# Batch 1's scores in float16 halves, batch 0's last 64 rows of two heads in one tile, and a new order

## The chip, the cores and the metric

The kernel runs on one core of one Trainium2 chip. The metric is device time in microseconds (us) of one execution. TensorE (PE) multiplies, VectorE (DVE), ScalarE (ACT) and GpSimd (POOL) work on tiles, and SyncE (SP) issues the transfers.

## The reference

```python
def _attn_ref(q, k, v):                       # each (4, 12, 448, 64) float32
    scores = 1.0 / np.sqrt(64) * np.matmul(q, k.transpose(0, 1, 3, 2))
    scores = np.where(np.triu(ones((448, 448)), k=1), -1e9, scores)
    scores = scores - np.max(scores, axis=-1, keepdims=True)
    attn = np.exp(scores)
    attn = attn / (np.sum(attn, axis=-1, keepdims=True) + 1e-09)
    return np.matmul(attn, v)

x = attn_out.transpose(0, 2, 1, 3).reshape(1792, 768)
r = np.maximum(x @ w_in, 0.0)                 # w_in (768, 2048)
out = (r * r) @ w_out                         # w_out (2048, 768)
```

Causal attention of 4 batches and 12 heads over 448 rows of 64 columns, then a feed-forward layer with a squared relu on all 1,792 rows.

## The kernel before

**Halves.** Most products run in float16 on values that are split in a high and a low half, three products for one (high by high, high by low, low by high). Scaling by powers of two from norms keeps the halves in range. `hi` (L478) writes a high half, as a rule on ACT (L485), `lo` (L491) the low half on DVE (L498). `pow2` (L508) makes a power of two and its inverse from a norm with four tiny DVE operations.

**Weights.** `load_wi` and `load_wo` (L999, L1006) bring w_in in 24 tiles and w_out in 16. `narrow` (L1011) repacks each on DVE in three operations (L1015, L1018, L1021). Gram matmuls of the packed tiles on PE (L1054, L1103; L1107 is the one of w_out) give the scale, `scale_out` (L1119) the scales of w_out, and then the halves are split (`split_pe` L1025, `split_w` L1038). The six tiles of one quarter of w_in's columns end in `widest` (L1066): a reduction (L1067) and a scaling of the identity (L1068) on DVE, then a matmul and a second reduction.

**Attention of batch 0** is `early` (L841), in float32: part 0 has the rows 0 to 255 in two chunks of 128, part 1 the rows 256 to 447 in two chunks of 96. For each of six pairs of heads q and k are transposed by PE (L877), scores (L898), the masked minimum with its accumulator on DVE (L906, a custom operation and the reading of its accumulator), exp on ACT (L910), normalisation, transposes (L938), weighted values (L954). Part 1 has 4 pieces for each pair, 352 or 448 columns wide.

**Attention of batches 1 to 3** is `pair` (L685), in four query chunks of 112 rows (`P`). Batches 2 and 3 split q and k in halves in the buffer `qs` and transpose them by transfers (L703) into `qk`; L770 are their scores, L753 their masked minima, L757 their exp. Batch 1 works in two parts of two chunks: `part_load` (L602) loads rows of q, k and v into `raw`; PE transposes q and k in float32 (L724, with `ident`), ACT copies them back over `raw` (L656); L784 are the float32 scores. In all batches but 0 the exponentials are split in halves in `psrc`, transposed by transfers (L678) into `pt`, and L816 are the weighted values with v's halves in `vp`, three products for two heads. L836 on POOL copies columns of the result `xt` for the next batch's blocks.

**Norms.** `vnorm` (L543) squares seven tiles `vn` of a batch's v on ACT (L552), with an accumulator. `pair_norm` does q and k of batches 2 and 3.

**Feed-forward.** `sub_block` (L1250) takes 256 or 128 rows: `prepare` (L1159) computes row norms (squares on ACT, L1168; the six pairs' squares added on DVE in three steps, L1171; the sum over columns on PE, L1174), the first layer is L1269, relu and square L1224 to L1233, the second layer L1287 in `second_layer` (L1278), with L1299 and L1310 scaling the results. Batch 0's two blocks are the phase "n", of 256 and 128 rows; the others are phase "m"; batch 3 goes through `products_block` (L1345).

**Order.** Nothing runs as it stands in the code. Each operation is added to a `Plan` (L94) with the tiles it reads and writes, one or more engines it can run on with a price, and a due time from the table PR (L23 to L77) by phase. `Plan.order` (L193) then schedules the list: whichever operation can start and is due first, on the engine that ends it first. `emit` (L290) writes the instructions in this order, so each engine's queue and SP's queue of transfers come from it. The code adds in this order: `early(0)`, `weights_in`, `early(1)`, `weights_out`, the blocks of batch 0, `attention(1)`, the blocks of batch 1, and so on (L1646 to L1671).

## Time and profile before

| | us |
|---|---|
| median of 3 runs (lowest, highest) | 618.01 (617.45, 620.81) |
| the profiled execution | 618.39 |
| its span | 616.7 |

| engine | busy us | share of the span |
|---|---|---|
| PE, matmuls | 597.9 | 97% |
| PE, weight loads | 442.2 | 72% |
| DVE | 497.4 | 81% |
| ACT | 428.6 | 69% |
| POOL | 9.7 | 2% |

The profile is one execution. Busy times are averages over stages that have different limits, so the windows of time further down are more telling. PE's matmuls are pipelined: the time of a group is best read from its start to the start of the next group. A weight load (PEld) overlaps matmuls. SP's rows show when transfers were issued, not how long they ran; the DMA share is the mean busy share of the core's 16 DMA engines.

### The profile page before, as it was taken

The page shows a single profiled execution, that of the slowest core. Times are in us where ns is not written, and L with a number is a line of the kernel's source. Part 1 is how long each engine was busy: PE and PEld are TensorE (multiplying, and loading weights), DVE is VectorE, ACT ScalarE, POOL GpSimd, SP SyncE. Part 2 cuts the span into 40 slices and gives each one's busy share as a digit, 9 for nine tenths or more (in the row PEclk, how much of TensorE's full clock was granted, in tenths as well). Part 3 has the DMA queues.
Part 4 walks back from the last instruction along what each step waited for, and adds up shares of the span by engine and source line. Part 5 has one row for each costly group of instructions (what it writes and reads, how often), then busy time and mean ns, then how long its engine had stood idle before and what let it go on. Part 6 is the DMA issues. An engine that isn't in the chain of part 4 may idle for free. (4 is left out here: it accounts for less than half of the span.)

```text
span 616.7 us, 13783 instructions
## 1 busy us (share of the span) xinstructions
PE 597.9 (97%) x5178; PEld 442.2 (72%) x5178; DVE 497.4 (81%) x1405; ACT 428.6 (69%) x1112; POOL 9.7 (2%) x21
## 2 busy tenths in 40 slices
PE   6888999999999999999999999999999999999997
PEld 4555778898566577868678668788966778886664
DVE  3799999999797798998889968889998999861000
ACT  4898999986798789577688869898934346451000
POOL 0000000001100000000000000000000000000000
PEclk9999999999999999999999999999999999999999
DMA  8965575765469788867789686775520000000000
GB/s 199 369 187 162 173 274 178 241 223 177 108 129 173 144 192 149 161 154 166 178 177 167 126 204 140 159 158 113 124 69 27 14 14 14 2 1 26 27 27 26
DMA packets 190914, 82.48 MB, mean 134 GB/s; under 512 B 177792, under 2 KB 185728, under 8 KB 190848
## 3 DMA queue, kind: packets, MB, share of 16 engines
q1 hardware_dynamic: 190704, 81.52, 53.7%
q8 instruction: 40, 0.66, 0.5%
q14 instruction: 26, 0.21, 0.1%
q10 hardware_dynamic: 144, 0.10, 0.0%
HBM read 47.19 MB, written 5.51 MB: 85 GB/s over the span
## 5 line engine op out<-in xcount | busy, mean ns | idle before, releaser
L1287 PE MATMUL bank<-wo,g 128*128 128x384 f16 x1056 | 182.2, 326 | 0.0
L1269 PE MATMUL bank<-xt,wi 128*128 128x256 f16 (+1 forms) x1728 | 169.1, 255 | 0.3 <-DVE xt L1191 0.3
L1269 PEld LDWEIGHTS <-wi 128*128 128x128 f16 x1728 | 144.6, 98 | 16.5 <-DVE psrc L498 0.7
L1287 PEld LDWEIGHTS <-g 128*128 128x128 f16 x1056 | 101.6, 98 | 63.0 <-issue 1.2
L757 ACT ACTIVATE pq<-bank,nm 112x336 f32<-112x336 f32 (+3 forms) x144 | 69.6, 492 | 14.6 <-DVE nm L753 14.0
L498 DVE SCALAR_TENSOR_TENSOR psrc<-pq,nm,psrc 112x112 f16<-112x112 f32 (+3 forms) x144 | 68.6, 506 | 8.4 <-ACT psrc L485 7.3
L485 ACT ACTIVATE psrc<-pq,nm 112x112 f16<-112x112 f32 (+3 forms) x144 | 67.0, 526 | 9.8 <-DMA pt<-psrc 6.9
L1310 DVE SCALAR_TENSOR_TENSOR ob<-bank,fac,ob 128x384 f32<-128x384 f32 (+1 forms) x27 | 16.1, 599 | 53.7 <-PE bank L1287 52.4
L1299 ACT ACTIVATE ob<-bank,fac 128x384 f32<-128x384 f32 x26 | 15.0, 576 | 59.3 <-PE bank L1287 59.1
L753 DVE CUSTOM_DVE_ANT_0 bank<-bank,mask,sc 112x112 f32<-112x112 f32 (+3 forms) x96 | 45.4, 512 | 7.0 <-PE bank L770 4.9
L816 PEld LDWEIGHTS <-vp 112*64 112x64 f16 x504 | 23.8, 109 | 12.4 <-issue 8.8
L770 PE MATMUL bank<-qk 128*112 128x112 f16 (+3 forms) x192 | 31.7, 285 | 0.7 <-ACT pq L757 0.6
L493 DVE TENSOR_TENSOR g<-r,g 128x512 f16<-128x512 f32 x44 | 30.1, 684 | 2.6 <-ACT g L485 2.4
L816 PE MATMUL bank<-pt,vp 112*64 112x224 f16 (+3 forms) x504 | 31.2, 268 | 0.6 <-DMA pt<-psrc 0.5
L1233 ACT ACTIVATE r<-r 128x512 f32<-128x512 f32 x40 | 24.9, 626 | 9.2 <-DVE r L1228 9.0
L1514 PEld LDWEIGHTS <-wi 128*128 128x128 f16 x288 | 28.1, 98 | 4.2 <-ACT g L1555 0.4
L757 ACT ACTIVATION_READ_ACCUMULATOR pq<-bank,nm 112x1 f32 x144 | 29.2, 203 | 0.0
L485 ACT ACTIVATE g<-r 128x512 f16<-128x512 f32 x44 | 27.0, 624 | 2.2 <-PE bank L1287 1.8
L906 DVE CUSTOM_DVE_ANT_0 bank<-bank,mask 128x128 f32<-128x128 f32 (+3 forms) x48 | 21.5, 487 | 4.3 <-PE bank L898 4.0
L898 PE MATMUL bank<-wo 64*96 64x256 f32 (+4 forms) x144 | 21.1, 389 | 2.8 <-ACT wo L656 2.0
L770 PEld LDWEIGHTS <-qk 128*112 128x112 f16 x192 | 19.8, 130 | 4.9 <-issue 1.1
L498 DVE SCALAR_TENSOR_TENSOR qs<-raw,sc,qs 112x512 f16<-112x512 f32 x24 | 17.3, 747 | 4.6 <-ACT qs L485 4.6
(189 smaller groups left out, 1023.2 us busy)
## 6 DMA issues: line engine op xcount, KB each, us to landing
raw<-in_moe_w_out_dram SPq DMA_DIRECT2D x8, 768.0 KB, 5.3
xt<-in_moe_w_out_dram SPq DMA_DIRECT2D x8, 768.0 KB, 4.6
xt<-in_moe_w_in_dram SPq DMA_DIRECT2D x11, 512.0 KB, 4.8
out_dram<-ob SPq DMA_DIRECT2D x25, 192.0 KB, 1.9
raw<-in_moe_w_in_dram SPq DMA_DIRECT2D x9, 512.0 KB, 5.4
vn<-in_v_dram SPq DMA_DIRECT2D x21, 192.0 KB, 3.8
raw<-in_v_dram SPq DMA_DIRECT2D x18, 224.0 KB, 3.2
raw<-in_q_dram SPq DMA_DIRECT2D x12, 224.0 KB, 3.4
```

The lines of the kernel that those rows point to most:

```text
L485: nc.scalar.activation(out=o, in_=i, func=ACTF.Copy, scale=s)
L493: return plan.add({"dve": dve_ns(n), "pool": pool2_ns(n)}, lambda e: engines[e].tensor_tensor(out=out(), in0=in_(), in1=top(), op=ALU.subt ...
L498: nc.vector.scalar_tensor_tensor(out=out(), in0=in_(), scalar=scale(), in1=top(), op0=ALU.mult, op1=ALU.subtract)
L753: one("dve", dve_ns(w, 1, 2 if F16S[b] else 1) - 10, lambda e: nc.vector.tensor_tensor_reduce(out=s.ap[0:P, 0:w], in0=s.ap[0:P, 0:w], in1= ...
L757: one("act", act_ns(w, True, 1, True), lambda e: nc.scalar.activation(out=p32[j].ap[0:P, b0 * P:b0 * P + w], in_=s.ap[0:P, 0:w], func=ACTF ...
L770: nc.tensor.matmul(out=s.ap[0:P, 0:(c + 1) * P], lhsT=qT.ap[:, j * NCH + c, :], rhs=kT.ap[:, a:a + c + 1, :].rearrange("p a t -> p (a t)") ...
L816: nc.tensor.matmul(out=pv.ap[j * D:(j + 1) * D, ca * P:t1], lhsT=vp.ap[:, hv, vb:vb + D], rhs=pT[j].ap[0:P, hp * ns + x:hp * ns + x + w, : ...
L906: one("dve", dve_ns(w, 1, 1) - 10, lambda e, c=c, j=j, w=w, ss=ss, nm=nm: nc.vector.tensor_tensor_reduce(out=ss[j].ap[0:M, 0:w], in0=ss[j] ...
L1233: nc.scalar.activation(out=r.ap[:, 0:n], in_=r.ap[:, 0:n], func=ACTF.Square)
L1269: nc.tensor.matmul(out=h.ap[:, y * n:(y + 1) * n], lhsT=wi_hl(ci, hw)[:, mc], rhs=x[:, kd, hx, off:off + n], start=(kd == 0 and hw == 0 an ...
L1287: nc.tensor.matmul(out=o.ap[:, 0:HALF], lhsT=gsl(kf, hg, tt * 128, (tt + 1) * 128), rhs=wo_hl(kf, hw)[:, hh * HALF:(hh + 1) * HALF], start ...
L1514: nc.tensor.matmul(out=ps.ap[:, y * n:(y + 1) * n], lhsT=A[0](f, kd, hw)[:, mc], rhs=B[0](kd, hx), start=(first and y == 0 and kd == 0 and ...
```

## The change

- **Batch 1's scores.** q and k of a pair are scaled by one power of two for all of q and one for all of k (`QK_UP`) and split in halves into `qs`; one transposing transfer for a pair and part brings both back into `raw`, 1,024 columns wide for the first part and 1,536 for the second, 12 in all. The scores are three float16 products. The PE transposes, ACT's copies and the float32 scores of batch 1 go. The loads of q and k are cut in smaller pieces.
- **Norms of batch 1.** `gram_norms(1)` loads q, k and v of batch 1 once more in 21 tiles and multiplies 63 blocks of 128 by 128 on PE; `vnorm(1)` goes.
- **Batch 0's last 192 rows.** A chunk of 128 rows for each head, 384 columns wide, and the last 64 rows of both heads stacked in one tile of 128 rows, 448 wide, with a mask of its own: 18 pieces for 24.
- **Small steps.** The low halves of batch 1's v are made on POOL, two operations each. In `widest` one multiplication replaces a reduction and a scaling. Scales of w_out that DVE made go to ACT. The squares of batch 0's blocks are summed by six matmuls instead of additions on DVE. Some results are staged in `xt` rather than in `qs`.
- **Order.** All of PR is new, and with it the order of the whole program. FIRST goes from 0 to 4: the first four loads of w_in have a due time of their own.

The core of the diff (PR, the cutting of the loads and the buffers left out):

```diff
-    FIRST = 0
+    FIRST = 4
-    KEYS = [(0, 128), (128, 128), (256, 96), (352, 96)]
+    KEYS = [(0, 128), (128, 128), (256, 128), (384, 64)]
...
+    def gram_norms(b):
...
+        for n, a in enumerate((q, k, v)):
...
+                    for z in range(w // 128):
+                        nc.tensor.matmul(
+                            out=ps.ap[:, n * 128:(n + 1) * 128], lhsT=top[:, z * 128:(z + 1) * 128], rhs=top[:, z * 128:(z + 1) * 128],
+                            start=(pr == 0 and z == 0), stop=(pr == NV - 1 and z == w // 128 - 1))
...
-                def turn(e, n=n, t=t, nch=nch):
-                    for c in range(nch):
-                        nc.tensor.transpose(t.ap[:, c * P:(c + 1) * P], (full(n) if nch == 4 else wide(n))[0:P, c], ident[0:P, 0:P])
...
-                one("pe", nch * 97, turn, raws[n][1] + ["ident"], [t], due)
-                copy(nch * P, lambda n=n: turned(n), lambda t=t, nch=nch: t.ap[:, 0:nch * P].rearrange("p (c t) -> p c t", t=P),
-                     [t], raws[n][1], due)
...
+                hi(nch * 128, lambda half=half: half(0), src, up, keys + [("vup", 1)], [(s_, n, 0)], due)
+                lo(nch * 128, lambda half=half: half(1), src, up, lambda half=half: half(0), keys + [("vup", 1), (s_, n, 0)], [(s_, n, 1)], due, keys)
+            o = at_[0][0] * 512 + at_[0][1] * 256
+            one("sp", {1024: 1540.0, 1536: 2200.0}[a], lambda e, a=a, o=o: nc.sync.dma_start_transpose(
+                out=raw[:, o:o + a // 2].bitcast(F16).rearrange("p (b t) -> p b t", t=128)[:, :, 0:P], in_=s_.ap[0:P]),
...
-                    for j in range(2):
-                        r = slice(j * D, (j + 1) * D)
-                        nc.tensor.matmul(
-                            out=ss[j].ap[0:P, 0:(c + 1) * P], lhsT=turned(0)[r, c - c0], rhs=turned(1)[r, 0:c + 1], start=True, stop=True)
+                    for z, (hq, hk) in enumerate(((0, 0), (0, 1), (1, 0))):
+                        for j in range(2):
+                            r = slice(j * D, (j + 1) * D)
+                            nc.tensor.matmul(
+                                out=ss[j].ap[0:P, 0:(c + 1) * P], lhsT=turned(0)[r, c - c0, hq], rhs=turned(1)[r, 0:c + 1, hk],
+                                start=(z == 0), stop=(z == 2))
...
-        T0, M, N = (0, 128, 256) if part == 0 else (256, 96, 192)
+        T0, MS, N = (0, (128, 128), 256) if part == 0 else (256, (128, 64), 192)
...
-            [], keys, ("wi", i - 60 * (i < FIRST), "wl"), 400.0, extra=1700.0)
+            [], keys, ("wi", i, "wl" if i >= FIRST else "wf"), 400.0, extra=1700.0)
...
+        for pr in range(0, NPAIR, 2):
+            one("act", act_ns(2 * n), lambda e, pr=pr: nc.scalar.activation(
...
+        for a, w, z in ((0, 3, 3), (0, 1, 1), (0, 1, 2)) if phase == "m" else ():
...
+        sums = 1 if phase == "m" else NPAIR
```

Three places of the new order. **At the start**, SP's queue of transfers (`wo` holds batch 0's q, k and v at this time, `g`, `xt` and `raw` are staging for w_in), before:

```order
L848 DMA wo<-in_k_dram 128x4x64 x2
L848 DMA wo<-in_q_dram 128x8x64 x2
L848 DMA wo<-in_k_dram 128x8x64 x2
L848 DMA wo<-in_v_dram 96x4x64 x2
L848 DMA wo<-in_v_dram 96x8x64 x2
L1002 DMA g<-in_moe_w_in_dram 128x1024 x4
L1002 DMA xt_140<-in_moe_w_in_dram 128x1024 x3
```

and after:

```order
L926 DMA wo<-in_k_dram 128x4x64 x2
L1118 DMA g<-in_moe_w_in_dram 128x1024 x3
L926 DMA wo<-in_q_dram 128x8x64 x2
L926 DMA wo<-in_k_dram 128x8x64 x2
L1118 DMA g<-in_moe_w_in_dram 128x1024
L1118 DMA xt_140<-in_moe_w_in_dram 128x1024 x3
L1118 DMA raw<-in_moe_w_in_dram 128x1024 x3
```

Three loads of w_in went ahead of q and k of the heads 4 to 11, and the rest of the first ones ahead of the later rows of v.

**Behind the last Gram matmul of w_out** (L1107 before, L1218 after), PE's queue, before:

```order
L1107 MATMUL bank_128<-wo 128x128
L1287 LDWEIGHTS g
L1287 MATMUL bank_120<-wo,g 128x384
L1287 LDWEIGHTS g
L1287 MATMUL bank_120<-wo,g 128x384
```

and after (L861 are batch 1's scores, L1385 the first layer):

```order
L1218 MATMUL bank_128<-wo 128x128
L861 LDWEIGHTS raw
L861 MATMUL bank_104<-raw 112x112
L861 LDWEIGHTS raw
L861 MATMUL bank_108<-raw 112x112
...
L1385 LDWEIGHTS wi
L1385 MATMUL bank_120<-xt_139,wi 128x128
```

Batch 1's first scores follow at once, and first-layer matmuls of batch 0's second block, which stood ahead of this place before, now follow it. Counted in the two programs: ahead of this place stood 288 first-layer matmuls of 256 columns, 288 of 128 and 54 second-layer ones; now 288, 90 and 24.

**POOL's queue**, where L836 alone worked in batch 1's attention before, has after:

```order
L526 TENSOR_SCALAR raw<-raw,vst 112x2x128
L528 TENSOR_TENSOR vp<-raw,vp 112x256
L914 TENSOR_SCALAR xt_140<-xt_139 128x2x64
...
L526 TENSOR_SCALAR raw<-raw,vst 112x512
L528 TENSOR_TENSOR vp<-raw,vp 112x512
```

L526 and L528 make a low half of v; there are twelve such couples, six of 256 columns and six of 512.

## Rows read from the trace of the kernel before

**Rows 1.** Windows: from:to, length, busy PE, PEld, DVE, ACT, POOL, PEclk, DMA share, GB/s
```profile
0.00:20.00 20.00, 13.77 (x64) 9.21 (x64) 5.92 (x33) 10.27 (x31) 1.38 (x9) 1.00 0.91 236
20.00:156.20 136.20, 130.08 (x1296) 101.23 (x1293) 134.33 (x358) 122.09 (x312) 4.77 (x6) 1.00 0.66 215
156.20:260.00 103.80, 101.61 (x881) 71.42 (x878) 88.83 (x281) 83.87 (x234) 0.37 (x1) 1.00 0.76 150
260.00:616.70 356.70, 352.40 (x2946) 260.34 (x2945) 268.36 (x737) 212.33 (x537) 3.23 (x6) 1.00 0.42 92
```

**Rows 2.** Timeline of PE at the last Gram matmuls: start, duration, line, out<-in
```profile
153.90 1.17 PE L1269 MATMUL bank<-xt,wi 128*128 128x128 f16 x18
154.90 1.14 PE L1287 MATMUL bank<-wo,g 128*128 128x384 f16 x6
155.88 0.51 PE L1107 MATMUL bank<-wo 128*128 128x128 bf16 x6
```

**Rows 3.** Timeline of PE in batch 1's scores, and weighted values of a later batch
```profile
167.71 0.83 PE L784 MATMUL bank<-raw 64*112 64x112 f32 x8
168.47 2.12 PE L1287 MATMUL bank<-wo,g 128*128 128x384 f16 x12
...
237.28 0.55 PE L724 MATMUL bank<-ident,raw 112*128 112x112 f32 x4
237.67 2.13 PE L1269 MATMUL bank<-xt,wi 128*128 128x256 f16 x18
239.73 1.57 PE L784 MATMUL bank<-raw 64*112 64x336 f32 x8
241.24 1.20 PE L816 MATMUL bank<-pt,vp 112*64 112x224 f16 x24
...
284.17 1.62 PE L816 MATMUL bank<-pt,vp 112*64 112x448 f16 x24
285.72 0.87 PE L770 MATMUL bank<-qk 128*112 128x336 f16 x4
```

**Rows 4.** Groups of DVE by shape: busy us, mean ns of one | idle before
```profile
L906 DVE CUSTOM_DVE_ANT_0 bank<-bank,mask 96x448 f32<-96x448 f32 x12 | 7.3, 640 | 0.0
L906 DVE CUSTOM_DVE_ANT_0 bank<-bank,mask 96x352 f32<-96x352 f32 x12 | 6.1, 542 | 0.0
...
L1171 DVE TENSOR_TENSOR sq<-sq 128x768 bf16<-128x768 bf16 x6 | 3.4, 568 | 0.0
...
L906 DVE DVE_READ_ACCUMULATOR2_ANT nm<- 96x1 f32 x24 | 3.3, 139 | 0.0
...
L1067 DVE TENSOR_REDUCE wst<-bank 128x1 f32<-128x128 f32 x4 | 1.1, 277 | 0.0
```

**Rows 5.** Timeline of DVE, the first narrowing, with its wait in brackets
```profile
18.01 0.43 DVE L1015 TENSOR_SCALAR wi<-g 128x512 int32<-128x512 int32 x1 [0.37 <-DMA g<-in_moe_w_in_dram]
```

**Rows 6.** Timeline of PE, two matmuls with 112-column weight loads and the next
```profile
288.39 0.26 PE L770 MATMUL bank<-qk 128*112 128x112 f16 x2
288.50 2.13 PE L1269 MATMUL bank<-xt,wi 128*128 128x256 f16 x18
```

**Rows 7.** Timeline of POOL beside DVE; POOL's L836 (min/median/max); a DVE group
```profile
287.38 0.74 DVE L498 SCALAR_TENSOR_TENSOR vp<-raw,vst,vp 112x512 f16<-112x512 f32 x1
287.62 0.66 POOL L836 TENSOR_SCALAR xt<-xt 128x128 f16<-128x128 f16 x1 [131.05 <-DVE xt L832]
...
L836 POOL TENSOR_SCALAR xt<-xt x12: 300/662/1080, 147.7 to 360.3; 128x128 f16<-128x128 f16 x12
...
L498 DVE SCALAR_TENSOR_TENSOR vp<-raw,vst,vp 112x256 f16<-112x256 f32 x6 | 2.8, 482 | 1.7 <-ACT vp L485 1.7
```

**Rows 8.** A window, SP's timeline in it, and landing times of L678's transfers
```profile
250.00:260.00 10.00, 10.00 (x106) 8.66 (x103) 9.26 (x22) 4.59 (x8) 0.00 (x0) 1.00 0.94 168
...
257.82 2.69 SPq L703 DMA_TRANSPOSE qk<-qs  x2
...
DMA to landing us min/median/max: 2.4/4.0/5.7
```

More of the change, by code (lines that the diff above doesn't have):

```diff
@@ L390, in attention_relu2_kernel, with n_ob @@
     b_ob = maker("ob", 2)
-    n_ob = lambda more, i: plan.spot([("qs", i - 2, 0), ("qs", i - 2, 1)], qs[:, i - 2, 0:2 * HALF].bitcast(F32)) if more and i > 1 else b_ob([128, HALF], F32)
+    def n_ob(more, i):
+        if more and i > 1:
+            prs = range(3 * i - 6, 3 * i - 3)
+            return xt[0][:, prs[0]:prs[-1] + 1, 0, 0:256].bitcast(F32), [("xt", 0, pr, 0) for pr in prs]
+        ob = b_ob([128, HALF], F32)
+        return ob, [ob]
     n_ss = maker("ss", 4)
@@ L712, in pair @@
             at_ = [place(pr, part, n) for n in range(3)]
-            raws = [(None, [("raw", z, h) for h in hs]) for z, _, hs in at_]
+            raws = [(None, [(k_, z, h) for h in hs for k_ in ("raw", "rawc")[:2 - (n > 0 and part)]]) for n, (z, _, hs) in enumerate(at_)]
+            nchs = [4 if part and n else 2 for n in range(3)]
             row = lambda n: raw[:, at_[n][0] * 512:(at_[n][0] + 1) * 512]
+            half_row = lambda n: row(n)[:, 0:512] if nchs[n] == 4 else row(n)[:, 256 * at_[n][1]:256 * (at_[n][1] + 1)]
@@ L730, in pair @@
+            raws[2] = (row(2)[0:P] if part else wide(2)[0:P], raws[2][1])
         z = None if whole or c0 else pr % 2
@@ new lines, in turned_qk @@
+            qkk = early_keys(0, part, pr) + early_keys(1, part, pr)
+            one("pe", 2 * 0.86 * sum(MS), turn, qkk + ["ident"], [t], due)
+            if part == 0:
+                copy(512, lambda: rows[:, :, part].rearrange("p n c t -> p c n t"),
+                     lambda t=t: t.ap.rearrange("p (c n t) -> p c n t", n=2, c=2), [t], qkk, due)
+                return rows, qkk
+            for c, M in enumerate(MS):
+                copy(2 * M, lambda c=c, M=M: rows[:, :, part, c, 0:M],
+                     lambda t=t, c=c, M=M: t.ap[:, 256 * c:256 * c + 2 * M].rearrange("p (n t) -> p n t", n=2),
+                     [t], early_keys(0, part, pr, (c,)) + early_keys(1, part, pr, (c,)), due)
@@ new lines, in scored @@
+        def scored(pr):
+            rows, qkk = turned_qk(pr)
+            nm, sm = n_nm([128, 8], I32), n_sm([128, 8], I32)
+            if part == 0:
+                p32, pT = [[mk(j) for j in range(2)] for mk in (lambda j: n_ep(0, j, pr % 3), lambda j: n_eT(j, pr % 3))]
+                pieces = [(p32[j], (p32[j], c), [0, 128][c], 128 * (c + 1), 2 * j + c) for c in range(2) for j in range(2)]
+            else:
+                p32, pT = [n_ep(1, None, pr % 3)], [n_eT(None, pr % 3)]
+                pieces = [(p32[0], (p32[0], j), 384 * j, 384, j) for j in range(2)] + [(p32[0], (p32[0], 2), 768, 448, 2)]
+            held[pr] = p32, nm, sm, pT, pieces
@@ L898, in scores @@
                             nc.tensor.matmul(
[L899 to L900 removed]
+                                out=ss[j].ap[o, a:a + n_], lhsT=rows[r, 0, part, c, 0:MS[c]],
+                                rhs=rhs, start=(z == 0), stop=(z == len(blocks) - 1))
                 one("pe", mm32_ns(w) + 95, scores, qkk + [k_ for z in range(part) for k_ in early_keys(1, z, pr)], ss,
@@ L1173, in prepare, with total @@
                 [(sqs, i) for i in range(z, z + w)] + [(sqs, i) for i in range(a, a + w)], [(sqs, i) for i in range(a, a + w)], due, port=True)
-        one("pe", mm_ns(n), lambda e: nc.tensor.matmul(
-            out=tot.ap[:, 0:n], lhsT=ones_b, rhs=sq[:, 0, 0:n], start=True, stop=True), [(sqs, 0)], [tot], due)
+        sums = 1 if phase == "m" else NPAIR
+        def total(e):
+            for i in range(sums):
+                nc.tensor.matmul(out=tot.ap[:, 0:n], lhsT=ones_b, rhs=sq[:, i, 0:n], start=(i == 0), stop=(i == sums - 1))
+        one("pe", sums * mm_ns(n), total, [(sqs, i) for i in range(sums)], [tot], due)
         u, sg = n_u([128, SUB], I32), n_sg([128, SUB], F16)
@@ L1613, in attention @@
             return
+        vnorm(b)
         for i in pairs:
@@ L1630, in consts @@
             fill=-float(2 ** 100), base=0, channel_multiplier=1)
+        nc.vector.memset(mask2.ap[:, 0:384], 0.0)
+        for j in range(2):
+            h = slice(j * 64, (j + 1) * 64)
+            nc.gpsimd.tensor_copy(out=mask2.ap[h, 384:448], in_=mask[h, MZ + j * 64:MZ + (j + 1) * 64])
         nc.gpsimd.memset(ident, 1.0)
```

385 lines of the change are left out of this document (225 added, 160 removed), and 50 rows, old and new, of the table PR.

## The prediction, made before the changed kernel was run

> **What bounds the kernel now.** I read the windows first [rows 1], because what limits the kernel differs by stage. The column to compare is each engine's busy time against the window's length, and after it DMA's share. In the first 20 us DMA is at 0.91 while DVE works 5.92 us: everything waits for data. From 20 to 156.2 us DVE is busy 134.33 of 136.2, which makes it the bound, with PE (130.08) and ACT (122.09) behind it. From 156.2 on PE is the bound: 101.61 of 103.8 us, then 352.40 of 356.7, at a granted clock of 1.00 (the level of 2.4 GHz) throughout. I therefore cut the program at 156.2 us. There the last Gram matmul of w_out ends [rows 2], the last thing that the weights' preparation on DVE releases on PE. Ahead of this marker the time is set by when DVE gets through the weights and batch 0's softmax; behind it by how much PE work is left: 616.7 - 156.2 = 460.5 us.
>
> After that I read PE's timeline where batch 1's scores are computed [rows 3], DVE's groups by shape [rows 4], and for what can go wrong the first narrowing [rows 5], a 112-column weight load [rows 6], POOL beside DVE [rows 7] and the DMA share with the transposing transfers [rows 8].
>
> **PE behind the marker, what goes.** Batch 1 has six head pairs. Each has ten fp32 transposes, and four of them delay the next matmul by 237.67 - 237.28 = 0.39 us, 97 ns each [rows 3]: 60 x 97 = 5.8 us. Its fp32 scores come in two visits: the narrow widths cost 168.47 - 167.71 = 0.76 us, the wide ones 241.24 - 239.73 = 1.51 us [rows 3], so 2.27 x 6 = 13.6 us. Together 19.4 us.
>
> **What comes.** Three float16 products for two heads and four query chunks, widths 112 to 448: 24 matmuls a pair. The trace has a twin with the same widths and count, the weighted values of a later batch: 24 matmuls from 284.17 to 285.72, 1.55 us [rows 3]. 1.55 x 6 = 9.3 us. The twin splits the array by output columns, the new scores by input rows; the old fp32 scores split it by rows too, so overlap of the two heads is likely. If they did not overlap, 18 matmuls of 256 columns in 239.73 - 237.67 = 2.06 us [rows 3] give 0.45 ns a column, and 6 x 1,120 columns x 6 pairs would be 18.0 us. So the saving lies between 1.4 and 10.1 us; I take 10.1, the nearer row.
>
> Here is where a weight load could decide. Two matmuls with their own 112-column loads start at 288.39, and the next matmul starts 0.11 us later [rows 6]; such loads are thus mostly hidden. The Trainium skill, page "TensorE: Matmul & The Clock Gate", section "LDWEIGHTS (loading the stationary operand)", gives a load as columns / 1.2 ns, 93 ns for 112. If every load stood in line, 144 of them would take 13.4 us instead of 9.3, and the sum below would end 4.1 us later; the 0.11 us for two speaks against it here.
>
> **What moves.** The program's order shows PE work that stood ahead of the marker and now stands behind it: 198 first-layer matmuls of 128 columns and 30 second-layer ones of 384. Eighteen of the first take 154.90 - 153.90 = 1.00 us, six of the second 155.88 - 154.90 = 0.98 [rows 2]. 198 x 55.6 ns + 30 x 163 ns = 11.0 + 4.9 = 15.9 us more behind the marker. So the stretch behind it becomes 460.5 + 15.9 - 10.1 = 466.3 us, **5.8 us longer**. The change can pay only if the marker comes more than 5.8 us earlier.
>
> **DVE ahead of the marker.** The 24 softmax reductions of batch 0's last 192 rows cost 12 x 640 + 12 x 542 + 24 x 139 ns = 17.5 us [rows 4]. The 18 new ones are six of 448 columns and twelve of 384; with 640 for the first and 575 between the two rows for the second, 6 x 640 + 12 x 575 + 18 x 139 = 13.2 us: -4.3. The six additions of squares for batch 0's blocks go to PE: 768 columns take 568 ns [rows 4], and they have 1,920 columns in all: -1.4. Four reductions of 277 ns go [rows 4]: -1.1. Twelve tiny operations on the scales go to ACT, at some 139 ns: -1.7. Four low halves of q and k come ahead of the marker, 4 x 0.48 [rows 7], and three of g leave it, a little wider: nil. That is 8.5 us by durations. Neighbouring records overlap by some hundredths, so I take 8. DVE is 98.6% busy here, so this should come through, unless ACT or PE is the next one late. ACT is handed work (the scales, the new high halves) but loses batch 1's squares of v, which the 63 Gram matmuls replace. These cost PE 63 x 55.6 ns = 3.5 us, which the 15.9 us that left this stretch cover.
>
> **The start.** The w_in loads stand behind q and k of batch 0's first 256 rows and all of its v on the queue. The first narrowing waits for its load until 18.01 us [rows 5], and DVE idles 14 of the first 20 us [rows 1]. Three loads now go ahead of q and k of heads 4 to 11 and of the later rows of v, together 1.64 MB (from the shapes), 6.9 us at the 236 GB/s of this window. DVE then has weights to narrow in its gaps from about 11 us on. The price: these q and k loads land later by 3 x 0.26 MB, 3.3 us, so pairs two to five of batch 0 start later. The gain can be at most the idle left between 11 and 20 us, about 6, and nothing if DVE waits for q and k instead. I take 4. If there is a loss I expect it under 1 us, because DVE's queue has narrowing to do meanwhile.
>
> **The sum.** The marker comes 8 + 4 = 12 us earlier, at 144; the stretch behind it is 466.3 us. Span 616.7 - 12 + 5.8 = 610.5; the profiled execution took 618.39, 1.7 more than its span, so 612.2. The median of the runs shown (618.01) lies 0.4 below the profiled one: **611.8 us**, 1.0% faster. About 0.5% (3.1 us) is what a measurement of this kernel can tell from no change: faster means under 614.9, slower over 621.1.
>
> **Rivals.**
> 1. *The transfers become the bound (slower).* Twelve transposing transfers, six of 1,024 and six of 1,536 columns, join the queue in the stretch of batch 1's attention, where DMA is at 0.76 of 103.8 us, 78.9 us [rows 1]. In 250 to 260 us six of the smaller kind are issued (two queue operations a row, three such rows) at a share of 0.94 [rows 8]: at most 9.4 / 6 = 1.6 us each. 6 x 1.6 + 6 x 2.4 = 24 gives 103 of 103.8 + 5.8 = 109.6 us: it fits, barely. If each held the engines for the 4.0 us from issue to landing [rows 8], 78.9 + 48 exceeds the stretch by 17.3 us: 629. It decides from (109.6 - 78.9) / 15 = 2.0 us a smaller one. PE behind it can take first-layer work of batch 1's neighbours meanwhile, so a part is hidden.
> 2. *The relief doesn't bring the marker forward.* ACT is busy 122.09 of 136.2 us and PE 130.08 [rows 1]; if one of them, or the w_out loads, sets the marker, each us missing from the 12 is lost. Without any of it 611.8 + 12 = 624; slower from a marker less than 2.7 us earlier, within 0.5% up to 8.9.
> 3. *Only the start fails.* The marker is 8 us earlier: 616, no difference.
> 4. *POOL holds DVE up.* POOL gets 24 operations, the low halves of batch 1's v. The one POOL row beside a DVE operation took 0.66 us and ended as DVE's did (287.62 + 0.66 against 287.38 + 0.74), where the shortest took 300 ns for 128 columns [rows 7]: one waits for the other. At 300 ns per 128 columns they hold 12 x 0.6 + 12 x 1.2 = 21.6 us. DVE idles 15 us in the stretch [rows 1] and gains as much from new low halves as the stretch grows by (24 come, 12 go: 12 x 0.48 = 5.8). If all of it blocked DVE, 6.6 us would be lost: 618, no difference. The Trainium skill, page "SBUF — State Buffer", section "Who interferes with whom", says that a DVE operation with two SBUF inputs and a GpSimd one that reads SBUF block each other fully; the two ends above agree with it.
> 5. *The heads don't overlap on PE*, or weight loads show: 8.7 us lost at most, 620; no difference for most of that range.
>
> **How the numbers follow.** Forecast with its own spread of some 4 us either way (607 to 615): 0.56. Both relief terms better than taken (marker 14 us earlier and fewer gaps on PE, under 607): 0.06. Rival 1: 0.09, most of it slower. Rival 2: 0.13, two thirds of it slower. Rival 3: 0.06; rival 4: 0.05; rival 5: 0.05. Faster 0.62, within 0.5% 0.21, slower 0.17. The range leaves out the best 0.05 or so and the tails of rivals 1 and 2: 605 to 622.
>
> **What would show it.** The last Gram matmul of w_out near 144 us (rival 2: after 150); the first narrowing near 11 us; DVE still near 98% busy up to the marker; groups of score matmuls adding up to 1.55 us a pair (rival 5: 3.0); DMA under 0.95 in the stretch of batch 1's attention and PE at 98% there (rival 1: PE gaps that end with a transposing transfer); DVE operations lengthened beside POOL's (rival 4). I am wrong if the marker stays where it is, or if PE gets gaps behind it that were not there.

## The result, and the profile after

The changed kernel takes **625.12 us** (median; 624.98 to 627.77) against 617.73 (617.35 to 620.81) of the kernel before on the same chip: a ratio of **1.0119**, 95% interval 1.0077 to 1.0161. It is 7.4 us slower, where 611.8 was forecast. The profiled execution of after took 627.77 us with a span of 626.1, 2.65 more than the median; its granted clock was 0.995, that of its other executions 0.997 to 1.00.

The windows of after, cut as in [rows 1] at the end of the last Gram matmul of w_out, its "marker" (from:to, length, busy PE, PEld, DVE, ACT, POOL, granted clock, DMA share, GB/s):

```profile
0.00:20.00 20.00, 13.46 (x60) 8.62 (x62) 9.55 (x39) 9.07 (x27) 1.90 (x11) 1.00 0.90 243
20.00:153.60 133.60, 126.50 (x1143) 95.31 (x1139) 123.97 (x316) 108.33 (x260) 3.75 (x4) 0.99 0.73 228
153.60:260.00 106.40, 100.72 (x993) 71.88 (x991) 87.10 (x261) 87.22 (x237) 7.15 (x15) 0.98 0.79 166
260.00:626.10 366.10, 361.78 (x3051) 269.25 (x3048) 276.19 (x769) 220.64 (x546) 14.17 (x18) 1.00 0.45 97
```

Its PE timeline at the marker, as in [rows 2], and its DVE timeline at the first narrowing, as in [rows 5] (start, duration; in brackets the wait and what ended it):

```profile
153.31 0.51 PE L1218 MATMUL bank<-wo 128*128 128x128 bf16 x6
```
```profile
11.16 0.43 DVE L1131 TENSOR_SCALAR wi<-g 128x512 int32<-128x512 int32 x1 [2.04 <-DMA g<-in_moe_w_in_dram]
```

The marker, at the cut of [rows 1], came 2.6 us earlier (156.2 to 153.6), not 12, and the stretch behind it grew by 12.0 us (616.7 - 156.2 = 460.5 to 626.1 - 153.6 = 472.5), not by 5.8. All of these are of the one profiled execution, so the 2.65 us that it lies above the median are in them. DVE's account up to the marker, from the first two windows and [rows 1]:

| us | before | after | forecast |
|---|---|---|---|
| DVE work up to the marker | 140.25 | 133.52 | -8; came -6.7 |
| of it done in the first 20 us | 5.92 | 9.55 | +4; came +3.6 |
| DVE idle from 20 us to the marker | 1.87 | 9.63 | no change; came +7.8 |

-6.7 - 3.6 + 7.8 is the 2.6. Both gains of DVE were there, nearly in full. What they freed turned into DVE standing idle. What DVE waited for most, from 20 us to the marker of after (total us, times, longest us), and the longest of these waits:

```profile
DVE bank L975 <- PE bank L1006: 4.5, 5, 2.3
```
```profile
21.54 0.30 DVE L975 CUSTOM_DVE_ANT_0 bank<-bank,mask 128x128 f32<-128x128 f32 x1 [2.29 <-PE bank L1006]
```

L1006 are batch 0's scores, L975 their masked minima: DVE waits for scores five times. Its longest single wait, 2.86 us for ACT, is shown below with the Gram matmuls. The experiments ask what stands behind these waits. Markers of experiments below are the end of the last row of that kind: 155.88 + 0.51 = 156.4 us before, 153.31 + 0.51 = 153.8 after.

Groups of PE by shape that waited for a transfer behind the marker (busy us, mean ns | idle us before, and what ended it), first of before, then of after:

```profile
L816 PE MATMUL bank<-pt,vp 112*64 112x224 f16 x216 | 15.2, 261 | 0.5 <-DMA pt<-psrc 0.5
```
```profile
L894 PE MATMUL bank<-pt,vp 112*64 112x224 f16 x216 | 15.2, 262 | 2.9 <-DMA pt<-psrc 2.9
...
L894 PE MATMUL bank<-pt,vp 112*64 112x448 f16 x72 | 9.6, 360 | 0.6 <-DMA pt<-psrc 0.6
...
L861 PE MATMUL bank<-raw 64*112 64x336 f16 x36 | 3.8, 317 | 0.8 <-DMA raw<-qs 0.8
```

L861 are the new scores, which wait for the new transposing transfer (`raw<-qs`), and L894 (L816 before) the weighted values, which wait for the old one of the softmax weights (`pt<-psrc`).

### The profile page after: what moved, and what is told of

It reads as the page before. It is cut to its first block, busy times and chain, and to the rows that moved or that the text cites. A ratio compares the mean times of both kernels' runs of the same rounds, so it can differ in the third digit from the quotient of the medians.

```text
span 626.1 us, 13955 instructions
## 1 busy us (share of the span) xinstructions
PE 602.5 (96%) x5239; PEld 445.1 (71%) x5239; DVE 496.8 (79%) x1383; ACT 425.3 (68%) x1068; POOL 27.0 (4%) x47
## 4 chain that ended last, share of the span: by engine, by line
PE 63%; DMA 3%; DVE 2%; ACT 2%; issue 1%; DVEq 0%; SPq 0%
PE bank L1403 29%; PE bank L1385 17%; PE bank L1633 9%; PE bank L894 4%; PE bank L846 4%; DMA pt<-psrc 1%; DMA out_dram<-ob 1%; PE bank L861 1%; ACT pq L833 1%; DMA raw<-qs 1%; DVE bank L829 0%; ACT psrc L510 0%; DVE psrc L523 0%; ACT junk L577 0%; DVE qs L523 0%
## 5 line engine op out<-in xcount | busy, mean ns | idle before, releaser
L1385 PE MATMUL bank<-xt,wi 128*128 128x256 f16 (+1 forms) x1728 | 167.7, 256 | 0.7 <-ACT r L1342 0.7
L1385 PEld LDWEIGHTS <-wi 128*128 128x128 f16 x1728 | 145.0, 98 | 17.4 <-issue 2.2
L833 ACT ACTIVATE pq<-bank,nm 112x112 f32<-112x112 f32 (+3 forms) x144 | 69.5, 489 | 14.5 <-DVE nm L829 12.1
L523 DVE SCALAR_TENSOR_TENSOR psrc<-pq,nm,psrc 112x112 f16<-112x112 f32 (+3 forms) x144 | 66.9, 504 | 5.3 <-ACT psrc L510 5.0
L510 ACT ACTIVATE psrc<-pq,nm 112x112 f16<-112x112 f32 (+3 forms) x144 | 64.6, 523 | 4.7 <-DMA pt<-psrc 2.0
L829 DVE CUSTOM_DVE_ANT_0 bank<-bank,mask,sc 112x336 f32<-112x336 f32 (+2 forms) x96 | 45.7, 511 | 7.9 <-PE bank L846 7.0
L894 PE MATMUL bank<-pt,vp 112*64 112x224 f16 (+3 forms) x504 | 31.1, 268 | 3.5 <-DMA pt<-psrc 3.5
L894 PEld LDWEIGHTS <-vp 112*64 112x64 f16 x504 | 23.8, 109 | 13.8 <-issue 6.9
L846 PE MATMUL bank<-qk 128*112 128x336 f16 (+3 forms) x192 | 31.7, 284 | 0.0
L526 POOL TENSOR_SCALAR raw<-raw,vst 112x256 f32<-112x256 f32 (+1 forms) x12 | 8.7, 724 | 410.8 <-ACT vp L510 381.5
L1006 PE MATMUL bank<-wo 64*128 64x128 f32 (+4 forms) x168 | 23.1, 359 | 2.6 <-ACT wo L726 2.0
L846 PEld LDWEIGHTS <-qk 128*112 128x112 f16 x192 | 21.2, 130 | 5.0 <-DMA qk<-qk 0.3
L829 DVE CUSTOM_DVE_ANT_0 bank<-bank,mask,vst 112x112 f32<-112x112 f32 (+3 forms) x48 | 22.2, 512 | 0.8 <-PE bank L861 0.8
```

The costliest lines, as they stand in the source:

```text
L510: nc.scalar.activation(out=o, in_=i, func=ACTF.Copy, scale=s)
L523: nc.vector.scalar_tensor_tensor(out=out(), in0=in_(), scalar=scale(), in1=top(), op0=ALU.mult, op1=ALU.subtract)
L829: one("dve", dve_ns(w, 1, 2) - 52, lambda e: nc.vector.tensor_tensor_reduce(out=s.ap[0:P, 0:w], in0=s.ap[0:P, 0:w], in1=mask[0:P, MZ + P - ...
L833: one("act", act_ns(w, True, 1, True), lambda e: nc.scalar.activation(out=p32[j].ap[0:P, b0 * P:b0 * P + w], in_=s.ap[0:P, 0:w], func=ACTF ...
L846: nc.tensor.matmul(out=s.ap[0:P, 0:(c + 1) * P], lhsT=qT.ap[:, j * NCH + c, :], rhs=kT.ap[:, a:a + c + 1, :].rearrange("p a t -> p (a t)") ...
L894: nc.tensor.matmul(out=pv.ap[j * D:(j + 1) * D, ca * P:t1], lhsT=vp.ap[:, hv, vb:vb + D], rhs=pT[j].ap[0:P, hp * ns + x:hp * ns + x + w, : ...
```

## The experiments

Five questions, each with a theory and its opposite: do the new Gram matmuls hold PE's queue, do the transposing transfers hold it, does relief of DVE bring the marker forward at all, is the earlier start worth its 4 us, and does POOL hold DVE. Each marker is read from one execution. Names with a_ are edits of the changed kernel, with b_ of the kernel before. Ratios are against the kernel before.

### The Gram matmuls' loads

a_gram_free: the Gram matmuls read a constant tile, so that they wait for no load. a_gram_noload leaves out their 21 loads too.

```diff
-  lhsT=top[:, z * 128:(z + 1) * 128], rhs=top[:, z * 128:(z + 1) * 128],
+  lhsT=ones_b, rhs=ones_b,
```
```diff
-  one("sp", dma_ns(128 * w * 4, w * 4), lambda e, ...: nc.sync.dma_start(out=t.ap, in_=...), ...
+  one("sp", dma_ns(128 * w * 4, w * 4), lambda e: None, ...
```

> The changed kernel in the same order, but the 63 Gram matmuls of batch 1's norms read a resident tile of ones, so they wait for no load (the norms are not the true ones); the loads still run. Theory 1 (a Gram matmul that waits in PE's queue for its load stops the first layer behind it, and the clock falls): the marker comes 3 to 5 us earlier than 153.6 and the time falls to 620 to 622. Theory 2 (ahead of the marker the relief of DVE ends in the chain of batch 0's last rows): 624 to 626, no difference.

> As the one before, and the 21 loads for these norms are left out. If the loads' time on the queue and on the DMA engines delays w_out's loads, this is 2 to 4 us faster than with the loads; if not, the same within 1 us.

Measured: 620.97 us, 1.0057 [1.0036, 1.0079], marker 149.4; and 621.54, 1.0063 [1.0041, 1.0085], marker 149.3. By medians the wait costs 4.1 us of the time, where the interval just overlaps that of after (1.0077 to 1.0161); the loads themselves cost nothing that shows. PE's timeline at the first of these matmuls (L596), of after and then of a_gram_free:

```profile
122.58 0.52 PE L1218 MATMUL bank<-wo 128*128 128x128 bf16 x6
124.74 0.35 PE L596 MATMUL bank<-vn 128*128 128x128 bf16 x3 [1.64 <-DMA vn<-in_k_dram]
...
126.11 5.42 PE L1385 MATMUL bank<-xt,wi 128*128 128x256 f16 x36
131.36 0.51 PE L596 MATMUL bank<-vn 128*128 128x128 bf16 x6
```
```profile
121.28 0.52 PE L1218 MATMUL bank<-wo 128*128 128x128 bf16 x6
121.64 0.33 PE L596 MATMUL bank<-ones_b 128*128 128x128 bf16 x3
```

At the marker the two executions are 4.4 us apart. Of this, 122.58 - 121.28 = 1.3 us were there ahead of the wait, and 1.3 are first-layer matmuls that ran slower behind it (5.42 us for 36, above, against 4.09). In a_plain_copy (next part), whose Gram matmuls wait too, they ran at full pace:

```profile
124.59 0.35 PE L596 MATMUL bank<-vn 128*128 128x128 bf16 x3 [1.05 <-DMA vn<-in_k_dram]
...
125.67 4.09 PE L1385 MATMUL bank<-xt,wi 128*128 128x256 f16 x36
```

The wait stands in PE's queue ahead of w_out's Gram matmuls and of the first layer, and the engines that wait for PE stood still with it. ACT's timeline of after a few us later, and DVE's next wait:

```profile
129.60 0.60 ACT L1342 ACTIVATE r<-bank 128x512 f32<-128x512 f32 x1 [4.06 <-PE bank L1385]
```
```profile
131.05 1.02 DVE L523 SCALAR_TENSOR_TENSOR wo<-wo,wst 128x768 f16<-128x768 f32 x1 [2.86 <-ACT wo L510]
```

### The transposing transfers

a_plain_copy moves batch 1's q and k with plain transfers of the same tiles in the same places, so that they arrive untransposed; the second head's score matmuls then read 48 rows for 64. a_both is a_plain_copy and a_gram_free together.

```diff
-  nc.sync.dma_start_transpose(out=raw[:, o:o + a // 2].bitcast(F16).rearrange(...)[:, :, 0:P], in_=s_.ap[0:P])
+  nc.sync.dma_start(out=raw[0:P, o:o + a // 2].bitcast(F16), in_=s_.ap[0:P])
```

> The changed kernel in the same order, but the 12 transposing transfers of batch 1's q and k are plain copies of the same bytes from the same tile to the same place (the scores are not the true ones, and the second head's matmuls read 48 rows for 64). Rival 1 (the transposing transfers fill the DMA engines and delay the exponentials' transfers, so that PE waits at 190 to 201 us): PE's gaps between the marker and 260 us fall by 4 us or more and the time to about 621. If not: 624 to 626.

> The changed kernel in the same order with both edits: Gram matmuls of batch 1's norms on a resident tile, and plain copies for the 12 transposing transfers. If the two waits are separate losses they add up: 625.1 - 4.1 - 3.2 = 617.8. If the second only shows because the first came ahead of it: about 620.5.

Measured: a_plain_copy 621.88 us, 1.0079 [1.0051, 1.0106]; a_both 619.30, 1.0018 [1.0001, 1.0035], marker 150.0, and behind it 617.1 - 150.0 = 467.1 us. By medians the transposing kind costs 3.2 us alone, inside the intervals' overlap, and 1.7 where the Gram matmuls don't wait (a_gram_free against a_both), where the intervals just part. Read the other way, the Gram matmuls' wait costs 621.88 - 619.30 = 2.6 us where the transfers are plain, with intervals well apart. So the two cost 5.8 us together (625.12 to 619.30), and how they share it depends on which goes first. PE at the longest gap of this stretch, of after and then of a_plain_copy:

```profile
190.51 3.10 PE L1403 MATMUL bank<-wo,g 128*128 128x384 f16 x18
195.80 0.62 PE L894 MATMUL bank<-pt,vp 112*64 112x224 f16 x12 [2.19 <-DMA pt<-psrc]
196.35 4.78 PE L1403 MATMUL bank<-wo,g 128*128 128x384 f16 x18
201.06 0.63 PE L894 MATMUL bank<-pt,vp 112*64 112x224 f16 x12
```
```profile
192.54 0.63 PE L894 MATMUL bank<-pt,vp 112*64 112x224 f16 x12 [1.95 <-DMA pt<-psrc]
193.10 3.10 PE L1403 MATMUL bank<-wo,g 128*128 128x384 f16 x18
196.13 0.63 PE L894 MATMUL bank<-pt,vp 112*64 112x224 f16 x12
```

The gap is there with plain copies too (1.95 us). So it comes with something else in the change than the transposing of q and k: the new order, or twelve more transfers of whatever kind. No run separates these two. Only what stands behind the gap differs: 18 matmuls that take 3.03 us elsewhere (193.10 to 196.13) took 4.71 (196.35 to 201.06).

### POOL

a_lo_dve gives DVE the twelve low halves of v that POOL makes, as one operation each. By the trace of after these are not all batch 1's, as was said ahead of the prediction: the six couples of 256 columns run from 149.7 to 203.5 us and are batch 1's, the six of 512 columns run from 362.8 to 439.6 us and belong to batch 3's attention.

```diff
-  if e == "dve":
+  if e in ("dve", "pool"):
```

> The changed kernel in the same order, but the 12 low halves of batch 1's v are made by DVE (one operation each) at the place where POOL made them. Rival 4 (POOL's operations block DVE): 2 us or more faster than 625.1. Theory 1 and 2 (POOL costs DVE little): 0 to 4 us slower, since DVE has 7.4 us more to do.

Measured: 623.53 us, 1.0089 [1.0056, 1.0121]. By medians 1.6 us less, with an interval that overlaps that of after. This is a net figure: DVE has the twelve operations to do instead. That POOL's operations do lengthen DVE's shows in the traces. A tiny operation, L872, of after and then of a_lo_dve (ns min/median/max), and its longest beside POOL in after:

```profile
L872 DVE TENSOR_SCALAR nm<-sm x36: 155/164/885, 160.2 to 448.7; 112x4 f32<-112x4 f32 x36
```
```profile
L872 DVE TENSOR_SCALAR nm<-sm x36: 153/164/173, 156.8 to 442.3; 112x4 f32<-112x4 f32 x36
```
```profile
423.27 1.16 POOL L528 TENSOR_TENSOR vp<-raw,vp 112x512 f16<-112x512 f32 x1
423.57 0.89 DVE L872 TENSOR_SCALAR nm<-sm 112x4 f32<-112x4 f32 x1 [1.02 <-ACT pq L833]
```

### Relief of DVE

b_relief8 leaves out the third narrowing operation of every second w_out tile, 8.2 us of DVE close ahead of the marker; a_relief8 does so in a_gram_free. b_relief_in and a_relief_in leave it out for every second w_in tile instead (`n == 512`), 8.8 us between 18 and 100 us.

```diff
-  one("dve", dve_ns(n), lambda e: nc.vector.scalar_tensor_tensor(
+  one("dve", dve_ns(n), lambda e: None if n == DM and (next(skipped) % 2) else nc.vector.scalar_tensor_tensor(
```

> The kernel before with the third narrowing operation left out for every second tile of w_out: eight operations of 768 columns, 1.02 us each in the trace of after, so 8.2 us less DVE work ahead of the marker, and the order otherwise the same. If DVE alone sets the marker (as the prediction had it), the marker comes 8 us earlier and the time falls by about 8 us, to 610. If DVE, PE and ACT are a chain there, less than half of it arrives: 614 or more.

> The base with the third narrowing operation of every second tile of w_out left out: 8.2 us less DVE work ahead of the marker, as done to the kernel before. If DVE's work sets the marker in the changed kernel, the marker comes 6 to 8 us earlier: 613 to 615. If it is the chain through PE, ACT and DVE, 2 us or less: 619 to 621.

> The kernel before in its order, with the third narrowing operation left out for every second tile of w_in: twelve operations of 512 columns, about 0.73 us each, 8.8 us of DVE work between 18 and 100 us. Doing so for w_out's tiles (8.2 us between 100 and 156 us) moved the marker not at all. If DVE sets the pace in the first 100 us and not after, the marker comes 5 to 8 us earlier and the time falls to 610 to 613. If DVE's relief comes through nowhere because PE and ACT go in step with it: 615 to 618.

> The same in the changed kernel with Gram matmuls on a resident tile (base 621.0 us, marker 149.4). If DVE sets the pace in the first 100 us: marker at 142 to 144, 614 to 616. If the chain through PE's two score banks and ACT does: within 2 us of the base.

| | us | ratio | marker (before the edit) |
|---|---|---|---|
| b_relief8 | 614.95 | 0.9956 [0.9941, 0.9972] | 157.0 (156.4) |
| b_relief_in | 616.63 | 0.9982 [0.9968, 0.9996] | 156.5 (156.4) |
| a_relief8 | 620.58 | 1.0043 [1.0020, 1.0066] | 150.2 (149.4) |
| a_relief_in | 622.42 | 1.0080 [1.0056, 1.0104] | 150.9 (149.4) |

These four bear on the prediction's main step. The window up to the marker, of b_relief8 and then of b_relief_in, beside the second row of [rows 1]:

```profile
20.00:157.00 137.00, 131.78 (x1297) 102.73 (x1294) 128.13 (x350) 122.55 (x312) 3.77 (x6) 0.99 0.66 215
```
```profile
20.00:156.50 136.50, 130.73 (x1295) 101.49 (x1294) 128.43 (x344) 122.67 (x312) 5.89 (x6) 1.00 0.65 215
```

DVE is busy some 6 us less in both, and the marker is where it was: 137.0 - 128.13 = 8.9 us idle instead of 1.9. In time the four gain 2.7, 1.0, 0.4 and -1.5 us of 8.2 to 8.8 by medians (the last two against a_gram_free). What b_relief8 gains comes behind the marker, where PE idles 0.4 us of the 103.0 up to 260 us (before: 2.2 of 103.8):

```profile
157.00:260.00 103.00, 102.59 (x910) 73.03 (x908) 90.24 (x286) 84.32 (x235) 0.00 (x0) 1.00 0.74 152
```

Executions are apart before any edit acts. The same w_in Gram matmul of before and of b_relief8, whose programs differ only behind it:

```profile
60.94 0.40 PE L1058 MATMUL bank<-wi 128*128 128x128 bf16 x4
```
```profile
62.25 0.39 PE L1061 MATMUL bank<-wi 128*128 128x128 bf16 x4
```

So markers alone carry a spread of a us or more, and b_relief_in's is from the slowest of its ten executions, 2.7 us above their median. From this matmul to the marker before took 95.4 us and b_relief8 94.8: 0.7 us of 8.2 came.

### Relief of PE and ACT, alone and together

If not DVE, which engine? b_pe8 leaves out half of the first-layer matmuls of 128 columns of batch 0's second block (144, 8.0 us); b_pe_early8 72 of 256 columns between 62 and 103 us (8.0 us); b_act8 twelve squares of ACT (7.5 us). b_both8 is b_pe8 with b_relief8, b_pe_dve8 is b_pe_early8 with b_relief8, and b_all8 is all of b_pe8, b_relief8 and b_act8.

```diff
+  kds = KD // 2 if wide else KD                                     # b_pe8
+  kds = KD // 2 if phase == "n" and n == SUB and m < 8 else KD      # b_pe_early8
-  for kd in range(KD):
+  for kd in range(kds):
...
+  if phase == "n":                                                  # b_act8, in the squares
+      return
```

> The kernel before with half of the first-layer matmuls of batch 0's second block left out (144 of 128 columns, 55.6 ns each: 8.0 us of PE work ahead of the marker); the order otherwise the same. If PE alone sets the marker there (DVE's relief of 8.2 us in the run above moved it not at all), it comes 8 us earlier and the time falls to 610. If DVE and PE are both full and in step, it comes less than 3 us earlier and the time stays above 614.5.

> Both left out: 8.2 us of DVE work and 8.0 us of PE work ahead of the marker. If the two are in step, only now does the marker come 6 to 8 us earlier, and the time is 608 to 611. If a third engine or the loads set it, it comes less than 4 us earlier: above 613.

> The kernel before in its order, with the twelve squares of batch 0's blocks left out (ACT, 512 columns, 626 ns each: 7.5 us between 66 and 153 us; the relu then goes on unsquared). DVE's relief did not move the marker (157.0 and 156.5 for 156.4) and PE's by 0.8. If ACT sets the pace, the marker comes 5 to 7 us earlier and the time falls to 611 to 613. If the three engines are in step: less than 2 us, 616 to 618.

> The kernel before in its order with all three left out: 8.2 us of DVE work, 8.0 of PE and 7.5 of ACT ahead of the marker. If the three are in step (each alone 0 to 1 us, DVE and PE together 2.3), now the marker comes 5 to 8 us earlier: 609 to 613. If it is still above 153, something else sets it: the loads of w_out, or the latency from one engine to the next in the order as it stands.

> The kernel before in its order, with half of the first-layer matmuls left out in the first half of batch 0's first block: 72 of 256 columns, 111 ns each, 8.0 us of PE work, all between 62 and 103 us. In the traces whose chain of waits reaches back that far, 60 to 100 us is PE alone (40 of 40 us). If PE sets the pace there, the marker comes 4 to 8 us earlier and the time falls to 610 to 614. If not: within 2 us, 616 to 618.

> The same together with every second third-narrowing of w_out left out (8.2 us of DVE work between 100 and 156 us). If PE sets the pace from 60 to 100 us and DVE, with PE, from there to the marker, the two add: the marker 8 us or more earlier, 606 to 610. If the loads of batch 1's v on ACT's queue set it (as the chain at 115 to 143 us of the last two runs says): marker at 152 or later, above 612.

| left out of before | us | ratio | marker | from the matmul at 60.94 us of before to the marker (before: 95.4) |
|---|---|---|---|---|
| b_pe8: PE late | 619.25 | 1.0023 [1.0001, 1.0044] | 155.6 | 95.0 |
| b_pe_early8: PE early | 618.48 | 1.0027 [1.0007, 1.0048] | 155.8 | 95.1 |
| b_act8: ACT | 617.00 | 0.9986 [0.9972, 1.0001] | 155.7 | 95.7 |
| b_both8: PE late, DVE | 615.86 | 0.9970 [0.9953, 0.9987] | 154.1 | 92.6 |
| b_pe_dve8: PE early, DVE | 617.29 | 0.9990 [0.9976, 1.0005] | 156.8 | 94.6 |
| b_all8: PE late, DVE, ACT | 615.99 | 0.9983 [0.9969, 0.9996] | 154.4 | 94.6 |

No engine relieved by 8 us moves the marker by more than 0.8 us or shortens the way to it by more than 0.7. Two together shorten it by at most 2.8, three no further. With all three relieved none is busy all the time (window of b_all8), and the chain of work ahead of its marker runs over something else (start, duration, what):

```profile
20.00:154.40 134.40, 122.81 (x1148) 93.57 (x1147) 126.89 (x347) 116.59 (x300) 3.14 (x6) 0.99 0.67 221
```
```profile
134.32 3.15 DMA vn<-in_v_dram
...
137.55 0.62 ACT junk L552 x2
...
138.19 4.39 DMA vn<-in_v_dram
...
142.67 0.45 ACT junk L552
...
143.19 0.59 ACT r L1229
```

These are the loads of batch 1's v for its norms. ACT squares them, each stands in ACT's queue until its load is there, and the next load waits for a buffer (`vn` has two). Two loads and their squares take the chain from 134.32 to 143.12; ACT's work for the first layer stands behind them. The changed kernel squares no v of batch 1 on ACT, so this chain is one of the kernel before only. In b_pe_dve8 the chain names four such loads, 14.6 us in sum:

```profile
120.38 3.15 DMA vn<-in_v_dram
...
124.19 3.61 DMA vn<-in_v_dram
...
133.04 3.90 DMA vn<-in_v_dram
...
141.26 3.90 DMA vn<-in_v_dram
```

### The start, and the stacked tile

a_start is a_gram_free with the first three w_in loads, their narrowing and their Gram matmuls placed 7 us later again; b_start is the kernel before with these placed 7 us earlier. a_stack is a_gram_free without the part of batch 0's stacked tile's scores that goes over the first 256 columns.

```diff
+  t = at[i] + (7000.0 if i in self.late else 0.0)      # a_start; b_start: -
+  at[i] = max([t] + [at[d] + 1.0 for d in self.ops[i][2]])
...
+  if MS[c] == 64 and z == 0:                           # a_stack
+      continue
```

> The changed kernel in the same order and with Gram matmuls on a resident tile (621.0 us, marker at 149.4, the base of this and the next two), but the first three loads of w_in, their narrowing and their Gram matmuls put back behind q and k of heads 4 to 11, as before the change. If the earlier loads gained the 3 to 4 us that DVE is busier in the first 20 us, this is 3 to 4 us slower (marker at 153, 624 to 625). If DVE gave that back when it waited for the later q and k (2.3 us at 21.5), it is within 1 us of the base.

> The kernel before in its order, but the first three loads of w_in, their narrowing and their Gram matmuls 7 us earlier in the order, between the loads of q and k of heads 4 to 11. This part of the change alone. Taking the same part out of the changed kernel cost 4.9 us (marker 3.8 us later), so the marker should come 3 to 4 us earlier and the time fall to 613 to 615. If the gain needs the rest of the changed order, 617 to 619.

> The base with the 256-column part of the stacked tile's scores left out (batch 0's last 64 rows then miss 256 of their keys): some 0.5 us less for PE in each of six pairs, between the softmax pieces that share its two banks. If the stacked piece's turn on PE is what DVE waits for there (2.7 us in the trace of after), the marker comes 2 to 3 us earlier and the time falls to 618 to 619. If not: within 1 us of 621.0.

Measured: a_start 625.89 us, 1.0136 [1.0105, 1.0166], marker 153.2: 3.8 later than a_gram_free's and 4.9 us slower. Some of the 3.8 may be clock: from 30 to 35 us the granted clock was 0.56 in this execution, behind a wait of PE of 1.81 us, and 1.00 in a_gram_free's. b_start 619.04, 1.0027 [1.0013, 1.0040], marker 157.5: alone in the old order the same step gains nothing, it loses 1.4 us of the time. a_stack 619.45, 1.0038 [1.0020, 1.0056], marker 148.0: 1.4 earlier, no more than executions are apart; of the time 1.5, within overlapping intervals.

## Why the prediction was wrong, step by step

**The step that failed** is "DVE is 98.6% busy here, so this should come through, unless ACT or PE is the next one late". It took the busiest engine of [rows 1] for the one that sets the pace, and counted DVE's relief as time in full. The relief was there (6.7 us of 8), but DVE stood idle in its place: 1.87 us before, 9.63 after. Leaving 8 us of DVE out of the kernel before, in either of two places, left the marker at 157.0 and 156.5, against 156.4. Four queues run there in a fixed order: DVE's, busy 134.33 us of 136.2, PE's, 130.08, ACT's, 122.09 [rows 1], and that of the transfers, with the loads of v for which ACT waits. That they hold each other in turn is concluded from the relief runs, not shown wait by wait. PE and ACT were named in rival 2, "if one of them, or the w_out loads, sets the marker", at 0.13 and at 624 us; that rival deserved the larger chance. A busy 98.6% says that DVE has 1.9 us to spare. It doesn't say that the others have much: PE had 6.1, and a chain that changes engines can be as long as the window with no engine full.

Still, not all of the relief was lost. Where the Gram matmuls don't wait, DVE up to the marker of a_gram_free reads, with 9.37 us in the first 20:

```profile
20.00:149.20 129.20, 123.94 (x1143) 93.78 (x1139) 123.59 (x316) 108.36 (x260) 3.72 (x4) 1.00 0.75 237
```

At this cut the marker is 156.2 - 149.2 = 7.0 us earlier: 7.29 less work in all, 3.45 more of it in the first 20 us, 3.74 more idle. So there two thirds of DVE's gains came, in an order made new and with 15.9 - 3.5 = 12.4 us less of PE's work ahead of the marker by the prediction's prices. Which of these let them through was not tested.

**A term that was missing.** The 63 Gram matmuls were costed by their durations, 3.5 us. They stand in PE's queue behind loads of their own, and that wait costs 4.1 us (a_gram_free) or 2.6 (a_plain_copy against a_both). The prediction asked what waits behind the transfers of q and k, not what waits behind these.

**The stretch behind the marker**, +5.8 forecast, was right as a sum of work: with both causes of waiting gone it measures 467.1 us (a_both) against the forecast 466.3, and PE is busy 459.83 us of it:

```profile
150.00:617.10 467.10, 459.83 (x4039) 340.06 (x4038) 362.44 (x1027) 307.28 (x781) 22.07 (x34) 1.00 0.52 114
```

Before, PE was busy 101.61 + 352.40 = 454.0 us behind the marker, and 454.0 + 5.8 is 459.8. In after the stretch is 472.5, in an execution 2.65 us above the median where a_both's is 0.5 below. Of its terms:
- Scores: from start to next start over all pairs, 20.3 us of transposes and fp32 scores became 10.4; saved 9.9, forecast 10.1. A pair's narrow and wide groups, of which two show here, cost about 1.7 us (forecast 1.55):

```profile
189.88 0.69 PE L861 MATMUL bank<-raw 64*112 64x224 f16 x12
190.51 3.10 PE L1403 MATMUL bank<-wo,g 128*128 128x384 f16 x18
...
254.13 1.20 PE L861 MATMUL bank<-raw 64*112 64x336 f16 x12
255.26 1.92 PE L1385 MATMUL bank<-xt,wi 128*128 128x256 f16 x16
```

  0.63 and 1.13 us for twelve each. So rival 5 (heads that don't overlap, 18.0 us) did not come. The Trainium skill, page "TensorE: Matmul & The Clock Gate", section "LDWEIGHTS (loading the stationary operand)", would give 24 x 93 = 2.2 us a pair for loads that stand in line (an estimate from that page); the trace, with 1.76, speaks against their standing in line.
- Moved work: forecast 15.9; a_both's total bears the sum out, the term by itself was not measured.
- Rival 1, that transfers become the bound, came in small. PE's idle before the weighted values and the new scores grew from 0.5 to 4.3 us (2.9 + 0.6 + 0.8). Of the time 1.7 us (a_both) to 3.2 (a_plain_copy) is due to the transposing kind; most of the gaps stay with plain copies. The price of 24 us more on the DMA engines did not come: from the marker to 260 us they were busy 0.79 of 106.4 us, 84.1, against 78.9 before. (That price also counted two of the exponentials' transfers among its six.)

**The start** was right in its gain: first narrowing at 11.16 (forecast about 11) and 3.6 us more DVE work in the first 20 us (4). Its price was not: a loss "under 1 us" was expected, and DVE waited 2.29 us at 21.54 for the scores of batch 0, whose q and k now load later; a_start has no wait of DVE there. What is left of the gain at the marker is 3.8 by a_start, some of it perhaps clock. That it pays only within the new order (b_start) was not foreseen.

**POOL** (rival 4, 6.6 us at most): 1.6 net by medians (a_lo_dve), not clear of the intervals. Its sign, DVE operations lengthened beside POOL's, did show (L872), but the 24 operations were booked in one stretch, and half of them run in batch 3's. In sum they took 7.1 + 4.9 + 4.4 + 4.3 = 20.7 us, near the 21.6 that were costed.

**The account of the miss.** 625.1 - 611.8 = 13.3 us: 5.8 for the Gram matmuls' wait and the transposing kind together (a_both), and 7.5 left. a_both's span is 617.1, where 610.5 was forecast: its marker is 6.4 us earlier than before's, not 12, which makes 5.6, and the stretch behind it, cut at the marker's end in both, is 1.0 longer than forecast. The last 0.9 is that its median lies further above its span than was reckoned. The 5.6 are what did not arrive of the 12 us forecast for DVE's two gains, though the Gram matmuls no longer waited. A marker of one execution holds a us or more of spread, and so does this split.

**What stays open.** Which chain would set the marker once DVE, PE, ACT and the loads of v all have room was not tried, nor which one sets it in a_gram_free. Nor was an order planned anew around the relief: all runs keep the fixed order, and a plan that knew of the room might use it. The relief was taken from narrowing operations; the softmax operations that the change itself shortens stand at other places. No run that computes the whole result beat the kernel before.

## What to carry to other kernels

Before an engine's relief is counted as time, take the same microseconds out of it at the place in question, in a kernel that leaves work out, and see whether the stage ends earlier: here 8 us of DVE, of PE or of ACT, each alone, moved it by less than 1. Where several queues run in a fixed interleaved order and are all nearly full (here 90 to 99% busy), count a relief of one at a small part of its size until such a run says more. Of every added instruction ask what it waits for, not only how long it takes: 3.5 us of matmuls cost 2.6 to 4.1 more by standing ahead of others in PE's queue. And before two markers are compared, look at a point ahead of the edit in both executions: here b_all8 and b_relief8 were 2.5 us apart there.
